# A chunked linear-attention stage: two more key blocks transposed by TensorE, and the order of the stage planned anew

## The chip, the cores and the metric

The kernel runs on one core of a Trainium2 chip. The metric is the device time of one execution in microseconds; lower is better. Three executions of the kernel before took 582.23, 582.09 and 578.52 us, with a median of 582.09 us.

## What is computed

Three stages follow each other. The change lies in the first, a delta-rule linear attention over 2 batches, 8 heads, 768 steps and a head dimension of 48:

```python
k_n = k / (np.linalg.norm(k, axis=-1, keepdims=True) + 1e-06)
for t in range(S):
    y[:, :, t] = np.einsum('bhd,bhde->bhe', q[:, :, t], state)
    v_old = np.einsum('bhde,bhd->bhe', state, kt)
    state = state + bt * np.einsum('bhd,bhe->bhde', kt, vt - v_old)
```

Its output goes through a mixture of experts (8 experts; the gate and a local gate choose one expert for each token, `relu(x @ w1[e]) @ w2[e]`) and then through a mixer (the real part of two Fourier transforms, a normalization, and a two-layer network with a residual sum).

## The kernel before

**Blocks.** The 768 steps are cut into 24 chunks of 32 steps. Four chunks make a block (`hf` = 0 to 5 in the code), and two blocks make a group (`g` = 0 to 2). Every block holds all 16 batch-and-head pairs. Values are kept as two float16 tiles, a high part and a low part (`KBh`, `KBl`), so a product takes three matmuls (`mm3`, L310).

**What happens to a key block** (`prepK`, L270). The keys are normalized (`norm`, L231; VectorE scales them in L277), split into a high part by ScalarE (L224) and a low part by VectorE (L229) in `parts`, and each part is transposed into a tile `KT` of 128 x 2048 float16. `turn` (L164) does that in one of two ways. Either SyncE's queue issues one DMA transpose (L169), or `turn_pe` (L171) makes 16 TensorE transposes into PSUM (L177) in two halves and evicts each half by ScalarE (L180) or VectorE (L183). The table `TK` (L660) says which blocks go which way. VectorE then copies the transposed keys into a stacked form (`ST`, L308), TensorE forms the Gram matrix (`gram`, L313), and ScalarE evicts it (L323).

**The solve.** When both blocks of a group have their Gram matrices, `solve` (L346) transposes them in 32 x 32 pieces on VectorE (`Gu`, L362) and inverts a triangular system in 31 serial steps of two VectorE instructions each (L371, L373). A last VectorE transpose gives `PT` (L377).

**From the solve to the recurrence.** `prepT` (L381) splits `PT` into a high and a low part and copies these into block-diagonal tiles (`TBh`, `TBl`); a `split` (L325) is one ScalarE conversion (L333), one VectorE subtraction (L335) and eight copies, each by VectorE (L341) or ScalarE (L344). Only one split at a time can hold the buffer `ph`. TensorE multiplies `TB` with the keys into `W`, which ScalarE and VectorE evict (L403, L405). `prepV` (L408) and `prepQ` (L424) prepare values and queries; `prepQ` forms the masked query-key products `M` with the same `split`. Where the table `HOLD` is 1 it uses the `KT` tiles of `prepK`; for blocks 3 and 4 it transposes the keys a second time.

**The recurrence.** `chain` (L488) runs 24 steps for each of the two batches. A step needs `W` and `T` of its block: steps 0 to 7 those of group 0, steps 8 to 15 those of group 1, steps 16 to 23 those of group 2. ScalarE evicts the high part of the update `U` (L513), `low` (L535) makes its low part, either on VectorE (L543) or with one TensorE matmul (L546) and ScalarE (L550), and ScalarE and VectorE evict the state (L530, L556). `out` (L558) makes the outputs and sends them to memory, and `logits` (L602) the gate's scores.

**What sets the order.** The order of instructions on every engine is fixed when the kernel is built, by a planner (`Order`, L47). It simulates the engines with a cost in nanoseconds for every instruction (the number in each `yield`), and whenever a simulated engine is free it takes the waiting instruction of lowest rank. The ranks stand in the table `PR` (L662): `K2` is `prepK` of block 2, `T`, `V`, `Q` likewise, `s0` the solve of group 0, `n0` the normalization. The recurrence has rank 0, outputs rank 1, logits rank `LATE`. With `KEEN` and `SHARE` an engine may be held free: it does not take an instruction if another of a lower rank, at most `KEEN`, is due within `SHARE` times the first one's cost. Where two engines can do the same work, `pick` (L59) takes the one whose queue would let it end first by the planner's costs, to which an entry of `BIAS` is added: `BIAS[0]` for `low` on ScalarE, `BIAS[4]` for a split's copy on VectorE, `BIAS[7]` for an eviction of a transpose on VectorE, `BIAS[5]` and `BIAS[6]` for a load issued by ScalarE or GpSimd. Loads may be issued by ScalarE up to `BOTH` and by GpSimd up to `THREE`. A DMA transpose is planned with 2140 ns of SyncE's queue and with a landing time of 4000 ns behind its issue (L170). `LOADS` (L663) is the order of the loads: `k0`, `k1` are halves of the keys, `v0`, `v1` of the values, `w` the gate weights, `b` beta and `c` the constants. On the chip the engines follow the planned order and wait on semaphores.

Of the kernel before, what the change touches and what calls it, by code (L numbers as in the profile page):

```python
# [46 lines left out]
class Order:  # L47
# [40 lines left out]
    def run(s):  # L88
        while s.heap:
            t,_,x=heapq.heappop(s.heap)  # L90
            s.now=t
            if isinstance(x,str): s.grant(x); continue
            g,pr,y=x; s.pr=pr
            while True:
                if y is None: y=next(g,None)
                if y is None: break
                if isinstance(y,str):
                    if y not in s.flags:
                        s.wait.setdefault(y,[]).append((g,pr,None)); break
                elif y[0]=="+":  # L100
                    if not s.res[y[1]]:
                        w=s.wait.setdefault(y,[]); w.append((g,pr,None)); break
                    s.res[y[1]]-=1
                elif y[0]=="-":
                    w=s.wait.get(("+",y[1]))
                    if w:
                        z=min(w,key=lambda z: z[1]); w.remove(z); s.push(t,z)
                    else: s.res[y[1]]+=1
                elif y[0]=="!": s.set(y[1])
                elif y[0]=="":  # L110
                    if y[1]: s.push(t+y[1],(g,pr,None)); break
                else:
                    s.n+=1
                    heapq.heappush(s.q.setdefault(y[0],[]),(pr,s.n,g,y))
                    s.grant(y[0]); break
                y=None
        left={k:len(v) for k,v in s.wait.items() if v}
        assert not left,left

class Attn:  # L120
# [35 lines left out]
    def dma(s,out,in_,n=475):  # L156

        e=s.o.pick(("Q",n),*(("A",n+35+s.BIAS[5]),)*(s.o.now<s.BOTH),*(("P",1081+s.BIAS[6]),)*(s.o.now<s.THREE))
        yield {"Q":("Q",n,"H"),"A":("A",n+35,"H"),"P":("P",1081)}[e]
# [4 lines left out]
    def turn(s,out,in_,f,pe):  # L164

        if pe: s.o.add(s.turn_pe(out,in_,f),s.o.pr)
        else:
            yield ("Q",2140,0)
            s.nc.sync.dma_start_transpose(out=out,in_=in_.rearrange("p u d -> p (u d)"))  # L169
            s.o.add(s.arrive(f,4000))  # L170
    def turn_pe(s,out,in_,f):  # L171
        for i in range(2):
            r=slice(8*i,8*i+8)
            yield ("+","y")
            p=s.psC.tile([128,8,128],F16,tag="y",name="tp",bufs=2)
            yield ("T",440)
            for u in range(8): s.nc.tensor.transpose(p[:,u],in_[:,8*i+u],s.K["identh"])  # L177
            if s.o.pick(("A",1000),("V",1150+s.BIAS[7]))=="A":
                yield ("A",1000)
                s.nc.scalar.activation(out=out[:,r],in_=p,func=AF.Copy)  # L180
            else:
                yield ("V",1150)
                s.nc.vector.tensor_copy(out=out[:,r],in_=p)  # L183
            yield ("-","y")
        yield ("!",f)
# [84 lines left out]
    def prepK(s,hf,first):  # L270
# [11 lines left out]
        f=f"kT{hf}"  # L282
        yield from s.parts(KT,k,s.KBh[i],s.KBl[i],f,f"K{i}",s.TK[hf],"kT0" if hf==1 else None)
        yield ("!",f)
# [40 lines left out]
    def split(s,src,Bh,Bl,z):  # L325
# [10 lines left out]
        for q in range(4):  # L336
            r=slice(32*q,32*q+32)
            for t,B in ((hi,Bh),(lo,Bl)):
                if s.o.pick(("V",245+s.BIAS[4]),("A",640))=="V":
                    yield ("V",245)  # L340
# [83 lines left out]
    def prepQ(s,hf,first):  # L424
# [28 lines left out]
        else:  # L453
            yield ("+","KT")
            KT=[s.pk.tile([128,16,128],F16,tag=f"KT{j}",name=f"KT{j}",bufs=2) for j in range(2)]
            for X,B,x in zip(KT,(s.KBh,s.KBl),"hl"): yield from s.turn(X,B[hf%s.NB],f"kA{hf}{x}",s.TK[hf])
            for x in "hl": yield f"kA{hf}{x}"
# [77 lines left out]
    def low(s,b,c,x,uh,ul):  # L535

        nc=s.nc
        yield ("",600)
        if s.o.pick(("V",524),("A",480+400+s.BIAS[0]))=="V":
            yield ("V",524)  # L540
# [17 lines left out]
    def out(s,b,c,uh,ul):  # L558
# [34 lines left out]
        if hf==5: s.o.add(s.logits_end(b,c,yb),1)  # L593
        elif c8==3: s.o.add(s.logits(b,hf,yb),s.LATE)
        if c8==3:
# [55 lines left out]
    def rest(s):  # L651

        for f in ("ku3","G5","PT2","W43","W53","V4","V5","M4","M5"): yield f
        yield from s.after(s.o)
    BOTH=20000
    KEEN,SHARE=0,0.2
    LATE=20
    THREE=30000
    HOLD=(1, 1, 1, 0, 0, 1)
    TK=(1, 0, 0, 0, 0, 0)  # L660
    BIAS=(-355, -160, 902, 0, 281, 507, 387, 0)
    PR={'K0': 0, 'T0': 11.02, 'V0': 22.82, 'Q0': 10.02, 'K1': 4.12, 'T1': 15.34, 'V1': 12.1, 'Q1': 9.56, 'K2': 13.7, 'T2': 0, 'V2': 12.77, 'Q2': 26.59, 'K3': 7.84, 'T3': 35.68, 'V3': 7.09, 'Q3': 18.76, 'K4': 17.47, 'T4': 0, 'V4': 0, 'Q4': 4.01, 'K5': 55.99, 'T5': 17.02, 'V5': 23.22, 'Q5': 7.29, 's0': 9.74, 's1': 4.18, 's2': 11.55, 'n0': 0, 'n1': 8.98, 'n2': 14.57, 'lq': 5.83, 'lv': 3.01}  # L662
    LOADS="k0 w v0 b c k1 v1"  # L663
    def run(s):
        o=s.o
        s.clear()
        P=lambda n,d: s.PR.get(n,d)
        def loads():
            for n in s.LOADS.split():
                if n=="c": yield from s.load_consts()  # L670
                elif n=="w": yield from s.load_gates()
                elif n=="b": yield from s.load_beta()
                else: yield from s.load(n[0]+"p",int(n[1]))
# [59 lines left out]
class Rest:  # L733
# [687 lines left out]
    KEEN,SHARE=3,0.7  # L1421
# [22 lines left out]
IN=("q","k","v","beta","moe_w_gate","moe_w_local","moe_w1","moe_w2","moe2_w_ch1","moe2_w_ch2")  # L1444
LATE=("rc","upper","mirror")

def program(tc,I,y):
# [4 lines left out]
    def right(n): return pools(name=n,bufs=1,side="right",reuse_waits="tile")  # L1452
    with ExitStack() as st:
# [11 lines left out]
        with tc.manual_schedule():  # L1465
# [7 lines left out]
            def after(o):  # L1473
                eR.close()
                e,lp=right("late"); st.push(e)
                for n in LATE:
                    K[n]=lp.tile(list(I[n].shape),I[n].dtype,name=n)
# [54 lines left out]
```

## Time and profile before

| | |
|---|---|
| median of three runs | 582.09 us |
| the profiled execution's own time | 581.5 us |
| its span, first to last instruction | 579.7 us |
| VectorE (DVE) busy | 422.4 us (73%) |
| TensorE (PE) busy | 469.6 us (81%) |
| ScalarE (ACT) busy | 322.4 us (56%) |
| mean granted TensorE clock | 0.916 |

One execution is profiled. A span is the time from the first to the last instruction. The stretches are cut in microseconds from the span's start. An engine's idle time is put down to the instruction or transfer that released the instruction behind it. The attention's last instructions run at about 241 us; the experts and the mixer fill the rest.

### The profile page before, as it was taken

How to read it: one execution, taken by the hardware profiler on the slowest of the kernel's cores; microseconds unless marked ns; L12 is line 12 of the kernel's file. 1: busy time of each engine (PE TensorE's matmuls, PEld its weight loads, DVE VectorE, ACT ScalarE, POOL GpSimd, SP SyncE). 2: the span in 40 equal slices, each digit the busy share in tenths (PEclk: the TensorE clock that was granted, in tenths of full speed). 3: DMA queues.
4: the chain of work that ended last, by engine and by line, in shares of the span. 5: the costliest groups of instructions: out<-in, count | busy, mean ns of one | idle time of the engine just before them, and what ended most of it. 6: DMA issues, size and time to landing. Idle time of an engine off the chain costs nothing.

```text
span 579.7 us, 12919 instructions
## 1 busy us (share of the span) xinstructions
PE 469.6 (81%) x5172; PEld 373.2 (64%) x5172; DVE 422.4 (73%) x943; ACT 322.4 (56%) x729; POOL 78.6 (14%) x85
## 2 busy tenths in 40 slices
PE   0632026896599799679999999998899999999997
PEld 0531015885488688568888888887787655555575
DVE  7958989898999987479887979878987643231132
ACT  4654337897789998716766666762554332111111
POOL 6000000000000000040343332224111210000010
PEclk9975556997599999979999999999999999999999
DMA  7264035086105103839999997227100000010010
GB/s 250 57 126 119 5 68 74 9 185 132 36 3 103 29 3 91 308 103 356 387 302 321 352 305 246 104 70 267 58 0 1 28 2 1 0 55 0 1 55 27
DMA packets 66991, 67.23 MB, mean 116 GB/s; under 512 B 40086, under 2 KB 59483, under 8 KB 66928
## 3 DMA queue, kind: packets, MB, share of 16 engines
q1 hardware_dynamic: 63936, 57.59, 33.6%
q0 software_dynamic: 2992, 8.79, 4.7%
q8 instruction: 41, 0.67, 0.5%
q14 instruction: 22, 0.18, 0.1%
HBM read 51.95 MB, written 7.67 MB: 103 GB/s over the span
## 4 chain that ended last, share of the span: by engine, by line
PE 27%; issue 18%; POOL 5%; DVE 3%; DMA 1%; ACT 1%; POOLq 0%; ACTq 0%; SPq 0%
PE mp L1377 12%; PE mop L1403 12%; POOL xg L905 3%; POOL x2d L943 2%; PE fp L1243 1%; PE yp L1212 1%; DMA xa<-x2d 1%; PE up L1324 1%; DVE d L1131 1%; DVE zl L1196 1%; ACT zh L1194 0%; DMA x2d<-ot,sim 0%; DVE e L1131 0%; DVE Y L1269 0%; ACT un L1308 0%
## 5 line engine op out<-in xcount | busy, mean ns | idle before, releaser
L1387 DVE SCALAR_TENSOR_TENSOR ml<-mp,mh 128x256 f16<-128x256 f32 (+1 forms) x48 | 26.8, 557 | 81.0 <-ACT mh L1385 80.9
L1377 PE MATMUL mp<-uT,ws 128*128 128x256 f16 (+1 forms) x432 | 77.8, 326 | 0.0
L1403 PE MATMUL mop<-ws,mh 128*128 128x384 f16 x288 | 77.7, 326 | 0.0
L1385 ACT ACTIVATE mh<-mp 128x256 f16<-128x256 f32 (+1 forms) x48 | 23.5, 489 | 89.8 <-PE mp L1377 89.6
L934 PE MATMUL op<-ws,hh 128*128 128x384 f16 (+1 forms) x256 | 67.5, 326 | 0.0
L922 PE MATMUL hp<-xT,ws 128*128 128x240 f16 x576 | 64.6, 266 | 1.0 <-DVE xT L913 0.5
L312 PEld LDWEIGHTS <-KT 128*128 128x128 f16 x576 | 27.2, 117 | 52.8 <-issue 41.5
L922 PEld LDWEIGHTS <-ws 128*128 128x128 f16 x576 | 56.2, 98 | 6.9 <-issue 1.3
L1377 PEld LDWEIGHTS <-ws 128*128 128x128 f16 x432 | 42.2, 98 | 27.2
L898 DVE SCALAR_TENSOR_TENSOR ws<-raw,ws 128x1536 f16<-128x1536 f32 x32 | 55.9, 1749 | 0.0
L312 PE MATMUL ga<-ST,KT 128*128 128x64 f16 x288 | 16.8, 229 | 45.2 <-DVE ST L308 39.0
L895 ACT ACTIVATE ws<-raw 128x1536 f16<-128x1536 f32 x32 | 47.3, 1485 | 0.0
L1403 PE MATMUL mop<-ws,ml 128*128 128x384 f16 x144 | 46.9, 326 | 0.0
L934 PE MATMUL op<-ws,hl 128*112 128x384 f16 (+1 forms) x128 | 41.7, 326 | 0.0
L1403 PEld LDWEIGHTS <-mh 128*128 128x128 f16 x288 | 28.2, 98 | 17.8
L905 POOL DMA_INDIRECT xg<-xd,gm x16 | 22.0, 1377 | 114.7 <-DVE fl L1067 107.7
L934 PEld LDWEIGHTS <-hh 128*128 128x128 f16 (+1 forms) x256 | 29.1, 114 | 11.6
L373 DVE TENSOR_TENSOR P<-P,tmp 128x31 f32<-128x31 f32 (+15 forms) x93 | 31.5, 339 | 1.7
L371 DVE TENSOR_TENSOR tmp<-Gu,P 128x31 f32<-128x31 f32 (+15 forms) x93 | 31.2, 336 | 1.6
L925 DVE SCALAR_TENSOR_TENSOR hl<-hp,hh 128x480 f16<-128x480 f32 x32 | 21.0, 655 | 14.5 <-ACT hh L924 12.9
L943 POOL DMA_INDIRECT x2d<-ot,sim x16 | 19.6, 1228 | 87.5 <-ACT ot L939 85.0
L924 ACT ACTIVATE hh<-hp 128x480 f16<-128x480 f32 x32 | 18.1, 566 | 20.7 <-PE hp L922 18.4
(276 smaller groups left out, 1170.5 us busy)
## 6 DMA issues: line engine op xcount, KB each, us to landing
raw<-moe_w SPq DMA_DIRECT2D x64, 384.0 KB
x<-moe_w_ch SPq DMA_DIRECT2D x24, 384.0 KB
qp<-q SPq DMA_DIRECT2D x5, 512.0 KB
kp<-k SPq DMA_DIRECT2D x6, 384.0 KB
vp<-v SPq DMA_DIRECT2D x6, 384.0 KB
xd<-yb SPq DMA_DIRECT2D x48, 48.0 KB
xa<-x2d SPq DMA_DIRECT2D x6, 384.0 KB
ur<-x2d SPq DMA_DIRECT2D x2, 768.0 KB
```

The source lines that it names most:

```text
L312: s.nc.tensor.matmul(out=out,lhsT=st[l],rhs=mv[m],start=(first and i==0),stop=True,skip_group_check=True)
L371: nc.vector.tensor_tensor(out=x,in0=Gu[:,k,k+1:32].unsqueeze(2).to_broadcast([128,m,n]),in1=P[:,k,0:n].unsqueeze(1).to_broadcast([128,m,n] ...
L373: nc.vector.tensor_tensor(out=P[:,k+1:32,0:n],in0=P[:,k+1:32,0:n],in1=x,op=ALU.subtract)
L895: s.nc.scalar.activation(out=s.W[q][:,0].rearrange("p s c -> p (s c)"),in_=s.raw[q],func=AF.Copy,scale=WS)
L898: s.nc.vector.scalar_tensor_tensor(out=W[1],in0=s.raw[q],scalar=WS,in1=W[0],op0=ALU.mult,op1=ALU.subtract)
L905: nc.gpsimd.indirect_dma_start(out=s.xg[e][t][0:w],out_offset=None,in_=s.xd,in_offset=bass.IndirectOffsetOnAxis(ap=s.gi[0:w,8*t+e:8*t+e+1] ...
L922: nc.tensor.matmul(out=p[:,i],lhsT=s.W[q][:,a,i,128*k:128*k+128],rhs=xT[b][:,k],start=(n==0),stop=(n==8)); n+=1
L934: nc.tensor.matmul(out=s.po[t][0:w],lhsT=hs[a][:,i,128*t:128*t+w],rhs=s.W[q][:,b,i,384:768],start=(g==0 and i==0 and n==0),stop=(g==3 and ...
L943: i=s.nc.gpsimd.indirect_dma_start(out=s.x2d,out_offset=bass.IndirectOffsetOnAxis(ap=s.si[0:w,c:c+1],axis=0),in_=ot,in_offset=None,bounds_ ...
L1377: for k in range(3): nc.tensor.matmul(out=p,lhsT=s.w_ch1(a,k,f),rhs=s.uT[g][b][:,k,0:N],start=(n==0),stop=(n==8)); n+=1
L1387: nc.vector.scalar_tensor_tensor(out=hl,in0=p,scalar=0.0,in1=hh,op0=ALU.max,op1=ALU.subtract)
L1403: nc.tensor.matmul(out=pm[t],lhsT=hs[a][:,128*t:128*t+128],rhs=s.w_ch2(b,f),start=(f==0 and n==0),stop=(f==11 and n==2))
```

## The change

Blocks 1 and 2 are transposed by TensorE instead of by DMA (`TK`). The planned landing time of a DMA transpose becomes 7600 ns for block 0, 7000 ns for block 1 and 5000 ns for the others and for the second transposes in `prepQ`. The ranks, the biases, `KEEN`, `SHARE`, `LATE`, `BOTH` and the order of the loads get new values, so the planner writes another order for the attention. No instruction's form is new.

```diff
-            s.o.add(s.arrive(f,4000))
+            s.o.add(s.arrive(f,(7600,7000,5000)[min(int(f[2]),2)] if f[1]=="T" else 5000))
...
-    BOTH=20000
-    KEEN,SHARE=0,0.2
-    LATE=20
+    BOTH=10000
+    KEEN,SHARE=3,0.17
+    LATE=2
...
-    TK=(1, 0, 0, 0, 0, 0)
-    BIAS=(-355, -160, 902, 0, 281, 507, 387, 0)
-    PR={'K0': 0, 'T0': 11.02, 'V0': 22.82, 'Q0': 10.02, 'K1': 4.12, 'T1': 15.34, 'V1': 12.1, 'Q1': 9.56, 'K2': 13.7, 'T2': 0, 'V2': 12.77, 'Q2': 26.59, 'K3': 7.84, 'T3': 35.68, 'V3': 7.09, 'Q3': 18.76, 'K4': 17.47, 'T4': 0, 'V4': 0, 'Q4': 4.01, 'K5': 55.99, 'T5': 17.02, 'V5': 23.22, 'Q5': 7.29, 's0': 9.74, 's1': 4.18, 's2': 11.55, 'n0': 0, 'n1': 8.98, 'n2': 14.57, 'lq': 5.83, 'lv': 3.01}
-    LOADS="k0 w v0 b c k1 v1"
+    TK=(1, 1, 1, 0, 0, 0)
+    BIAS=(-968, -265, 917, 1203, 0, 646, 0, -72)
+    PR={'K0': 0, 'T0': 23.64, 'V0': 25.4, 'Q0': 5.26, 'K1': 3.26, 'T1': 3.87, 'V1': 23.15, 'Q1': 5.13, 'K2': 11.08, 'T2': 0, 'V2': 25.77, 'Q2': 20.56, 'K3': 17.27, 'T3': 42.07, 'V3': 20.29, 'Q3': 11.99, 'K4': 36.81, 'T4': 11.59, 'V4': 22.21, 'Q4': 3.06, 'K5': 9.48, 'T5': 7.31, 'V5': 24.68, 'Q5': 37.18, 's0': 27.62, 's1': 13.09, 's2': 20.94, 'n0': 2.59, 'n1': 22.39, 'n2': 14.57, 'lq': 0.11, 'lv': 4.13}
+    LOADS="k0 c b v0 w k1 v1"
```

## Rows read from the trace of the kernel before

**Rows 1.** Busy time by stretch: us, its length, then busy us (instructions) of each engine.

```profile
core 0: us, PE busy (x) PEld busy (x) DVE busy (x) ACT busy (x) POOL busy (x), PEclk, DMA share, GB/s
28.70:53.70 25.00, 5.72 (x100) 4.97 (x101) 17.23 (x38) 12.40 (x24) 0.00 (x0) 0.64 0.62 144
53.70:84.70 31.00, 5.63 (x94) 5.10 (x93) 28.61 (x77) 10.89 (x22) 0.95 (x1) 0.50 0.15 34
84.70:141.60 56.90, 42.43 (x812) 38.99 (x813) 51.69 (x133) 47.52 (x146) 0.00 (x0) 0.86 0.48 85
141.60:192.20 50.60, 39.93 (x746) 36.87 (x744) 47.09 (x125) 42.84 (x133) 1.23 (x1) 0.80 0.27 59
...
209.00:237.00 28.00, 26.88 (x571) 24.87 (x569) 19.62 (x62) 23.46 (x87) 0.00 (x0) 1.00 0.39 116
```

**Rows 2.** Timeline of VectorE: start, us, line, out<-in, count, idle before and releaser.

```profile
40.52 1.93 DVE L362 STREAM_TRANSPOSE Gu<-G 128x1024 f32<-128x1024 f32 x1 [0.79 <-ACT G L323]
...
81.01 1.25 DVE L377 STREAM_TRANSPOSE PT<-P 128x1024 f32<-128x1024 f32 x1
...
140.29 1.23 DVE L377 STREAM_TRANSPOSE PT<-P 128x1024 f32<-128x1024 f32 x1
...
190.93 1.25 DVE L377 STREAM_TRANSPOSE PT<-P 128x1024 f32<-128x1024 f32 x1
```

**Rows 3.** Timeline of ScalarE, first update with group 1 (step 8, both batches).

```profile
159.82 1.01 ACT L513 ACTIVATE U<-ups 64x96 f16<-64x96 f32 x4
```

**Rows 4.** Timeline of VectorE from 28.7 to 53.7 us, instructions with idle time before.

```profile
32.76 0.86 DVE L308 COPY ST<-KT 64x1024 f16<-64x1024 f16 x2 [4.06 <-DMA KT<-KBh]
34.33 0.86 DVE L308 COPY ST<-KT 64x1024 f16<-64x1024 f16 x2 [0.71 <-DMA KT<-KBl]
...
37.54 0.69 DVE L335 TENSOR_TENSOR pl<-am,ph 128x512 f16<-128x512 f32 x1 [0.49 <-ACT ph L333]
...
51.62 0.42 DVE L308 COPY ST<-KT 64x1024 f16<-64x1024 f16 x1 [1.22 <-DMA KT<-KBl]
```

**Rows 5.** Timeline of SyncE's queue: block 1's two DMA transposes.

```profile
24.37 1.73 SPq L169 DMA_TRANSPOSE KT<-KBh  x1
26.75 5.51 SPq L169 DMA_TRANSPOSE KT<-KBl  x1
```

**Rows 6.** Timeline: block 0's transposes on TensorE, their evictions by ScalarE and VectorE.

```profile
15.13 1.89 PE L177 MATMUL tp<-ca,KBha 128*128 128x128 f16 x16 [15.13 <-ACT KBha L224]
...
16.20 1.94 ACT L180 ACTIVATE KT<-tp 128x1024 f16<-128x1024 f16 x2 [0.40 <-PE tp L177]
...
21.02 0.63 DVE L183 COPY KT<-tp 128x1024 f16<-128x1024 f16 x1
```

**Rows 7.** Waits of VectorE from 84.7 to 141.6 us: us, times, longest.

```profile
DVE ST L308 <- DMA KT<-KBla: 1.2, 1, 1.2
```

**Rows 8.** Low parts on VectorE and split copies, up to 192.2 us: count, ns min/median/max.

```profile
L543 DVE SCALAR_TENSOR_TENSOR U<-ups,U x18: 243/256/261, 96.2 to 178.6; 64x96 f16<-64x96 f32 x18
...
L341 DVE COPY TBl<-pl x10: 274/284/290, 84.5 to 159.4; 32x512 f16<-32x512 f16 x10
...
L344 ACT ACTIVATE TBh<-ph x12: 612/627/629, 83.7 to 157.1; 32x512 f16<-32x512 f16 x12
L344 ACT ACTIVATE MBl<-pl x9: 608/612/628, 41.0 to 170.8; 32x512 f16<-32x512 f16 x9
L344 ACT ACTIVATE MBh<-ph x8: 625/626/629, 40.5 to 169.3; 32x512 f16<-32x512 f16 x8
L344 ACT ACTIVATE TBl<-pl x6: 608/626/630, 86.5 to 150.0; 32x512 f16<-32x512 f16 x6
```

**Rows 9.** Low parts on VectorE from 209 to 237 us; ScalarE's conversion for block 5.

```profile
L543 DVE SCALAR_TENSOR_TENSOR U<-ups,U x26: 239/256/261, 211.0 to 236.6; 64x96 f16<-64x96 f32 x26
...
206.11 1.08 ACT L333 ACTIVATE ph<-PT 128x512 f16<-128x512 f32 x1
```

## The prediction

> **What bounds the kernel now.** Read first the busy time by stretch. The attention ends at about 241 us, and everything behind it (routing, experts, mixer) keeps its code, so the question is when the attention ends. VectorE is busy 28.61 of 31.00 us, 51.69 of 56.90 and 47.09 of 50.60 in the three stretches from 53.7 to 192.2 us, but only 17.23 of 25.00 us from 28.7 to 53.7; behind 192.2 TensorE takes over (26.88 of 28.00 us from 209 to 237) [rows 1].
>
> Read next the landmarks on VectorE: the loop of 31 steps that solves a group of key blocks is one serial chain. Its first input is ready at 40.52 us, and the solved groups come at 81.01, 140.29 and 190.93 us, with the transposes of 1.23 to 1.25 us that end them [rows 2]. The state recurrence on the other engines waits for those: the first update that uses group 1 runs at 159.82 us, 18.3 us behind the end of its solve (140.29 + 1.23) [rows 2, 3]. So VectorE's own queue, up to the third landmark, sets the end: what it idles ahead of 192 us is lost, and what is taken off it is gained.
>
> Read last who made VectorE idle in the thin stretch. Block 1's DMA transposes: 4.06 us for the high half, 0.71 for the low half; block 2's low half: 1.22 us; behind block 1 come 0.49 us (ScalarE) and 0.79 us (the Gram matrix, on the first landmark's row) [rows 2, 4]. That is 7.27 of the 7.77 us that the stretch lacks (25.00 - 17.23). The high transpose of block 1 was issued at 24.37 us and its first reader started at 32.76, 8.4 us later [rows 4, 5]; the planner allowed 4.0.
>
> **The change part by part.**
>
> *Blocks 1 and 2 are turned by TensorE.* Four DMA transposes go. With them go the waits of block 1 (4.06 + 0.71) and block 2 (1.22): 6.0 us. Of the 1.28 us behind block 1 I take half, since the Gram matrix still has to be formed behind the last copy: together -6.6 us, between 0 (the wait returns in another form) and -7.3. SP's queue loses its part as well: the transpose at 26.75 us held it for 5.51 us [rows 5], and the second key load and the query loads behind it start sooner; nothing waits for these at that place, so I count nothing.
>
> What is added: four tiles, each 16 transposes. Block 0 shows the price: a tile took TensorE 1.89 us, ScalarE 0.97 us for one of the two evictions (1.94 for two), VectorE 0.63 us where it took one [rows 6]. TensorE's 4 x 1.89 = 7.6 us and ScalarE's part lie where these engines have room: 5.72 and 12.40 us busy of 25.00 [rows 1]. If that cover is gone the whole of a tile is on the path, 1.89 + 0.97 us. VectorE's part is on the path: one of block 0's four evictions was its own, so two of the eight: +1.3 us, between 0 and 8 x 0.63 = +5.0.
>
> For one 128x128 block the row gives 1.89/16 = 0.118 us. [...]
>
> *The planner's landing times* (4.0 us become 7.0 for block 1, 5.0 for the other blocks and the late key transposes). Only blocks 3 to 5 still use them for their first turn. Block 5's low half made VectorE wait 1.2 us [rows 7]; a plan that allows 5.0 instead of 4.0 puts other work there: -0.6 us, half of it, between 0 and -1.2.
>
> *The choice of engine.* The bias for the low part of U falls from -355 to -968: before, the planner saw 524 for VectorE and 525 for TensorE with ScalarE; now it sees 524 and -88. The bias for the copies of the splits falls from 281 to 0: VectorE's way looks 281 cheaper. The two pull VectorE in opposite directions. Ahead of 192.2 us VectorE makes 9 low parts (18 instructions of 0.256 us): at most -4.6 us. ScalarE makes 35 split copies there, which cost VectorE 0.28 us each: at most +9.9 us [rows 8]. The low's threshold moves by 613, more than the 0.51 us of a low, the copies' by 281, one copy's length: if 6 lows leave (-3.1) and 8 copies come (+2.3), the net is -0.8 and smaller than what I know of either; I take 0, and both ends for the range.
>
> *The ranks.* The first solve falls behind nearly everything (9.74 to 27.62). It runs in gaps already: from 40.52 to 81.01 us VectorE is all but full [rows 1, 2], so another order of the same work ends at the same time; 0. Block 4's T goes from first (0) to 11.59 and block 5's stands ahead of it at 7.31. Block 5's split cannot start before block 4's has released the buffer `ph`; what remains is a copy already running when block 4's tiles want the engine, half of a 0.63 us copy [rows 8], +0.3 us; if block 5's conversion goes first, the upper end is its 1.08 us [rows 9]. Logits move from rank 20 to 2. They use TensorE and ScalarE only, and the recurrence waits for a solve twice, so ahead of 192 us they are hidden by that wait; 0, without cover a share of the last stretch, which is the slow case below. The waiting rule (KEEN 3, SHARE 0.17) holds back an engine for a higher-ranked instruction that is due within 0.17 of the next one's length, less than before for rank 0, and new for ranks up to 3: 0. The constants are loaded second instead of last, and the ACT queue is open for loads only until 10 us: the first landmark needs block 1's chain, which the earlier constants don't shorten: 0.
>
> **Sum.** -6.6 + 1.3 - 0.6 + 0.3 = -5.6 us. The profiled execution took 581.5 us, so 575.9; the median of the three runs stands 0.6 above it (582.09), so **576.5 us**.
>
> **The rivals.**
>
> *The wait comes back on TensorE (no change).* Two tiles of block 1 and one eviction take 2 x 1.89 + 0.97 = 4.75 us if TensorE gets to them only when VectorE has run out of work, which is today's 4.06 + 0.71 = 4.77. For it: the low half is made last, so one tile at least is always behind it; and Gram matrices want TensorE at the same time. Against it: the high tile can be turned while VectorE makes the low half. With four evictions on VectorE (2.5): -1.2 - 0.6 + 2.5 - 0.6 + 0.3 = +0.4, 582.5 us.
>
> *VectorE is relieved too (a larger gain).* All 9 early low parts leave VectorE, few copies come, and the whole of the 1.28 us goes: -5.6 - 4.6 - 0.6 = -10.8, 571.3 us. For it: the low's bias moved most. Against it: ScalarE is 47.52 of 56.90 us and 42.84 of 50.60 us busy there [rows 1], so the planner will often find it occupied.
>
> *The new biases load the engine that is already full (slower).* In the last eight steps ScalarE is busy 23.46 of 28.00 us [rows 1], and all 13 low parts there (26 instructions) are VectorE's [rows 9]. Moved to ScalarE they cost 0.51 us each (1.01 us for two in rows 3), 6.6 us, while its idle time is 4.5 us of waits in a serial chain that need not shrink. It decides once more than 9 of the 13 move. With half of the 35 copies on VectorE ahead of that (+5.0): -5.6 + 6.6 + 5.0 = +6.0, 588.1 us. For it: the threshold of 613 is more than a low. Against it: the planner counts ScalarE's queue before it chooses.
>
> That the change doesn't do what it says has little room: blocks 1 and 2 keep their turned tiles for the queries, so no second DMA transpose of them is left.
>
> **How the numbers follow.** Forecast 0.40, no change 0.22, larger gain 0.22, slower 0.16. What this kernel's measurement can tell from no change is about 1%, 5.8 us; the forecast lies on that line, and I count 0.22 of it as faster and 0.18 as the same. Faster 0.22 + 0.22 = 0.44, same 0.18 + 0.22 = 0.40, slower 0.16. The range reaches past the larger gain (571.3) by the rest of its bound and stops inside the slow case: 569 to 587 us. The likeliest case's own range is 574 (no eviction on VectorE, block 5's wait and the waits behind block 1 gone: -1.3 - 0.6 - 0.7) to 580 (all eight evictions on VectorE: +3.7).
>
> **What would show it.** Right: no VectorE wait for a transposed tile between 28 and 52 us, the first landmark at 34 to 36 instead of 40.5 us, the third near 185, and the attention's end earlier by the same 5 to 6 us. Wrong in the first step: VectorE idles 4 us again, now for TensorE or an eviction. Wrong in the biases: VectorE's busy time up to the third landmark moves by more than 2 us. Slow case: ScalarE full and TensorE thinner in the last eight steps. All of it is wrong if the third landmark moves and the end does not, or if the stretch behind the attention changes its length.

## The result and the profile after

The changed kernel takes 585.41 us (median of 13 runs, 583.62 to 586.67) against 582.21 us for the kernel before (13 runs beside it): ratio 1.0057, 95% interval 1.004 to 1.0074. It is 3.2 us slower, where 5.6 us less was forecast. That is 0.6%, less than the 1% that I had named as the least that can be told from no change; but the interval leaves out 1, so the kernel is slower, if by little.

The profiled execution has a span of 584.0 us (before 579.7). Read the two attentions side by side first, cut at the same instructions: start of the first solve, ends of the three solves, first instruction of the routing behind the attention. The columns are those of [rows 1]. First the kernel before:

```profile
0.00:40.52 40.52, 13.74 (x200) 12.46 (x201) 30.62 (x63) 21.23 (x34) 10.53 (x27) 0.92 0.53 142
40.52:82.26 41.74, 6.98 (x120) 6.11 (x119) 38.84 (x98) 15.48 (x30) 0.00 (x0) 0.52 0.31 79
82.26:141.52 59.26, 42.35 (x810) 38.91 (x811) 52.95 (x135) 49.80 (x150) 0.95 (x1) 0.85 0.46 82
141.52:192.18 50.66, 39.99 (x747) 36.94 (x745) 47.12 (x125) 42.91 (x133) 1.23 (x1) 0.80 0.27 60
192.18:241.13 48.95, 43.32 (x893) 38.92 (x890) 35.63 (x105) 42.43 (x133) 0.00 (x0) 1.00 0.35 108
```

Then the kernel after, the same view:

```profile
0.00:43.56 43.56, 17.31 (x228) 15.63 (x229) 34.34 (x68) 27.90 (x43) 9.19 (x23) 0.93 0.32 108
43.56:82.86 39.30, 8.77 (x159) 8.03 (x157) 37.54 (x99) 13.64 (x25) 0.00 (x0) 0.59 0.21 58
82.86:140.36 57.50, 41.87 (x762) 38.34 (x762) 50.60 (x127) 48.97 (x149) 0.95 (x1) 0.83 0.35 77
140.36:195.70 55.34, 42.89 (x807) 39.74 (x808) 50.55 (x134) 41.13 (x138) 0.95 (x1) 0.81 0.36 62
195.70:245.84 50.14, 45.70 (x896) 41.70 (x893) 30.99 (x89) 40.83 (x146) 0.00 (x0) 0.93 0.35 111
```

Add the first four rows. VectorE was busy 169.5 us up to the end of the third solve and idle 22.7 of 192.2; now it is busy 173.0 us and idle 22.7 of 195.7. So it has 3.5 us more work and no less idle time. (Another profile of before's order, below, idles 19.8 us up to there, so of the idle time this says only that it did not shrink.) The last row adds 1.2 us at a lower granted clock (0.93 for 1.00), and behind the routing's first instruction the two are alike (584.0 - 245.84 = 338.2 us, before 338.6). VectorE's landmarks, which answer to [rows 2], come 3.0 us later, 0.6 later, 1.2 earlier and 3.5 later. Two stretches grew, the first by 3.0 us and the third solve's by 4.7 (55.3 for 50.7), with VectorE busy 3.7 and 3.4 us more in them; the two between them shrank.

```profile
43.56 1.94 DVE L362 STREAM_TRANSPOSE Gu<-G 128x1024 f32<-128x1024 f32 x1 [0.44 <-ACT G L323]
...
81.61 1.25 DVE L377 STREAM_TRANSPOSE PT<-P 128x1024 f32<-128x1024 f32 x1
...
139.12 1.24 DVE L377 STREAM_TRANSPOSE PT<-P 128x1024 f32<-128x1024 f32 x1
...
194.45 1.25 DVE L377 STREAM_TRANSPOSE PT<-P 128x1024 f32<-128x1024 f32 x1
```

What VectorE waited for from 28.7 to 53.7 us, beside the last wait above, is the answer to [rows 4] (timeline of VectorE, after):

```profile
33.10 0.69 DVE L183 COPY KT<-tp 128x1024 f16<-128x1024 f16 x1 [3.26 <-PE tp L177]
...
35.00 0.42 DVE L308 COPY ST<-KT 64x1024 f16<-64x1024 f16 x1 [0.25 <-ACT KT L180]
```

No DMA is named any more, but 3.26 us stand where 4.06 stood: VectorE now waits for TensorE. The timeline of TensorE after shows why; it answers to the first row of [rows 6]:

```profile
27.18 1.03 PE L177 MATMUL tp<-ca,KBh 128*128 128x128 f16 x8 [1.73 <-ACT KBh L224]
29.90 1.03 PE L177 MATMUL tp<-ca,KBl 128*128 128x128 f16 x8 [1.68 <-DVE KBl L229]
30.72 1.48 PE L312 MATMUL ga<-SQ,KT 128*128 128x64 f16 x24
32.02 1.04 PE L177 MATMUL tp<-ca,KBh 128*128 128x128 f16 x8
32.86 1.05 PE L177 MATMUL tp<-ca,KBl 128*128 128x128 f16 x8
```

A tile of block 1 isn't turned in 1.89 us as block 0's was in before. Its second eight transposes wait behind the first eight of the other tile and behind query products of block 0, so the high tile takes from 27.18 to past 33 us. And both parts of block 1 come later than before. VectorE makes the low part, here in after and in before's order (the best version below, where L240 is L229):

```profile
28.82 1.02 DVE L229 SCALAR_TENSOR_TENSOR KBl<-kp,ca,KBh 128x768 f16<-128x768 f32 x1
```

```profile
25.90 0.99 DVE L240 SCALAR_TENSOR_TENSOR KBl<-kp,ca,KBh 128x768 f16<-128x768 f32 x1
```

The low part is done at 29.84 us in after. In before the DMA transpose that reads it was issued at 26.75 [rows 5], 3.1 us sooner. That is as much as the first solve is late (3.0 us).

VectorE's extra work is read from the groups by line and shape, up to the end of the third solve (busy us, mean ns). Before, then after:

```profile
L543 DVE SCALAR_TENSOR_TENSOR U<-ups,U 64x96 f16<-64x96 f32 x18 | 4.6, 253 | 0.2
L341 DVE COPY TBl<-pl 32x512 f16<-32x512 f16 x10 | 2.8, 283 | 0.2
L341 DVE COPY MBl<-pl 32x512 f16<-32x512 f16 x7 | 2.7, 390 | 0.1
L341 DVE COPY MBh<-ph 32x512 f16<-32x512 f16 x8 | 2.3, 282 | 0.2
L341 DVE COPY TBh<-ph 32x512 f16<-32x512 f16 x4 | 1.1, 285 | 0.1
```

```profile
L420 DVE SCALAR_TENSOR_TENSOR V<-vp,V 128x768 f16<-128x768 f32 x6 | 5.7, 944 | 0.0
L341 DVE COPY TBl<-pl 32x512 f16<-32x512 f16 x13 | 3.7, 283 | 0.3
L341 DVE COPY MBl<-pl 32x512 f16<-32x512 f16 x12 | 3.4, 284 | 0.3
L341 DVE COPY MBh<-ph 32x512 f16<-32x512 f16 x11 | 3.1, 282 | 0.2
L341 DVE COPY TBh<-ph 32x512 f16<-32x512 f16 x9 | 2.6, 286 | 0.3
...
L543 DVE SCALAR_TENSOR_TENSOR U<-ups,U 64x96 f16<-64x96 f32 x4 | 1.0, 255 | 0.3 <-ACT U L513 0.3
```

Seven low parts left (14 instructions, -3.6 us) and sixteen split copies came (29 to 45, +3.9). So the two choices of engine nearly cancel, +0.3 us. One more `V` (five before) adds 0.9 and one more eviction of a turned tile 0.8; these four make 2.0 of the 3.5 us. Three more memsets (L210) add 0.4, and one instruction of the normalization (L266) took 0.89 us for 0.24. All durations of VectorE up to there add up to 190.0 us, before 187.3; the rest of the 3.5 us is that consecutive instructions overlap less (17.0 us, before 17.8).

### The profile page after: what moved, and what is told of

The parts are those of the page before. It is cut to its first block, busy times and chain, and to the rows that moved or that the text cites. A ratio compares the mean times of both kernels' runs of the same rounds, so it can differ in the third digit from the quotient of the medians.

```text
span 584.0 us, 13058 instructions
## 1 busy us (share of the span) xinstructions
PE 479.5 (82%) x5255; PEld 383.2 (66%) x5255; DVE 420.6 (72%) x933; ACT 323.8 (55%) x750; POOL 77.5 (13%) x81
## 4 chain that ended last, share of the span: by engine, by line
PE 30%; issue 15%; POOL 5%; DVE 4%; ACT 1%; POOLq 0%; ACTq 0%
PE mp L1377 12%; PE mop L1403 12%; POOL xg L905 3%; POOL x2d L943 2%; PE fp L1243 2%; PE hp L922 1%; DVE ws L898 1%; PE yp L1212 1%; PE op L934 1%; PE up L1324 1%; DVE zl L1196 1%; DVE e L1131 0%; ACT zh L1194 0%; DVE d L1131 0%; ACT un L1308 0%
## 5 line engine op out<-in xcount | busy, mean ns | idle before, releaser
L312 PE MATMUL ga<-ST,KT 128*128 128x64 f16 x288 | 14.7, 217 | 36.5 <-DVE ST L308 33.2
L1403 PEld LDWEIGHTS <-mh 128*128 128x128 f16 x288 | 28.2, 98 | 17.8
```

What stands on the lines that cost most here:

```text
L312: s.nc.tensor.matmul(out=out,lhsT=st[l],rhs=mv[m],start=(first and i==0),stop=True,skip_group_check=True)
L1403: nc.tensor.matmul(out=pm[t],lhsT=hs[a][:,128*t:128*t+128],rhs=s.w_ch2(b,f),start=(f==0 and n==0),stop=(f==11 and n==2))
```

## The experiments

In the experiments marked *in place* the planner writes the same order as for its parent, and only the named instructions are changed when they are emitted. The other three are planned anew. A profile is one execution: before's order reaches the end of the third solve at 192.18 us in one profile and at 189.09 in another (the padded kernel below), while VectorE's busy time there differs by 0.2 us only. So I lean on busy times and on medians. Landmarks and idle times of single profiles differed by 3 us here with VectorE's work the same.

**The turn alone, in before's order** (in place).

```diff
+            s.o.add(s.turn_in_place(out,in_))        # f is kT1 or kT2: no dma_start_transpose
+    def turn_in_place(s,out,in_):
+        for i in range(2):
+            ...
+            for u in range(8): s.nc.tensor.transpose(p[:,u],in_[:,8*i+u],s.K["identh"])
+            yield ("",1000)
+            s.nc.scalar.activation(out=out[:,r],in_=p,func=AF.Copy)
```

> The kernel before with its order on every engine unchanged; only the four DMA transposes of blocks 1 and 2 are replaced, at the same place in the order, by 16 TensorE transposes and two ScalarE evictions each. Theory (turning on TensorE is worth it, the new order of the changed kernel loses it): block 1's tiles are there at about 27.5 and 30.5 us instead of 32.8 and 34.3, VectorE's waits of 4.06 + 0.71 + 1.22 us shrink to 2 us or less, the first solve starts near 37 us instead of 40.5, and the execution is 3 to 5 us shorter than the kernel before (577 to 579 us). Rival (turning on TensorE takes as long as the DMA transposes): the first solve starts within 0.7 us of 40.5 and the time stays within 1 us of the kernel before. Third reading (the 64 transposes and 8 evictions delay ScalarE or TensorE elsewhere): slower than the kernel before.

Measured: 580.6 us, ratio 0.9996 (0.9967 to 1.0026). The first solve starts at 38.16 us (before 40.52), the third ends at 188.05 (192.18), and the attention ends 3.5 us earlier. But the part behind it is 2.7 us longer (341.3 for 338.6): TensorE's conditional branch behind the routing, which skips the code for overflowing experts, took 3.69 us instead of 0.36.

> e1 (the order of before, blocks 1 and 2 turned by TensorE in place) with 24 instead of 20 filler products on TensorE ahead of the overflow branch, which also moves all later code of TensorE. In e1 the attention ended 3.5 us earlier but TensorE's branch took 3.69 us where the kernel before has 0.36, and the clock fell behind it. Theory (the branch's length is an accident of where TensorE's code stands or of the moment): the branch takes about 0.4 us again and the execution is 3 to 4 us shorter than the kernel before (578 to 579 us). Rival (an earlier end of the attention makes the branch wait for something that is not earlier): the branch ends at the same time as in e1, and the total stays within 1 us of e1.

Measured (`WARMR`, the fillers ahead of that branch, 20 to 24): 580.05 us, 0.9966 (0.9948 to 0.9985); the branch again 3.74 us. Moving it by eight matmuls changed nothing, so the theory as put there fell. I then counted TensorE's records up to the branch in every trace, which gave the next three.

```diff
-    WARMR=20
+    WARMR=16
```

> The order of before with blocks 1 and 2 turned in place, as in the earlier run, but with 16 instead of 20 fillers ahead of TensorE's branch behind the routing (8 matmuls less). Position theory: what the branch costs goes by how many instructions TensorE has had in front of it (its records up to the branch, weight loads included): 5,783 gave 0.35 us twice, 5,790 and 5,806 gave 3.7 us, 5,825 to 5,865 gave 0.46 us; in the two long ones the transfer of TensorE's next 16 KB of instructions starts 1.0 to 1.3 us behind the start of the branch, in the short ones it had been there, or the jump stayed in front of it. With 5,774 the branch takes 0.35 us and the kernel 3 us less than with 20 fillers: 577.3 us, 5 us below before. Rival (the branch is long because TensorE reaches it early, or because of the order): 3.7 us again and 580 to 581 us.

Measured: **576.83 us**, ratio 0.9923 (0.9898 to 0.9948), 4.5 us faster than before, and the best version of this study. The branch takes 0.35 us. The routing begins 4.6 us earlier (236.56 for 241.13 us) and the part behind its first instruction is as long as before's (338.2 for 338.6), so the gain lies in the attention and not in the four fillers fewer.

```diff
+            if hf==3 and c==3:
+                for _ in range(10): nc.tensor.matmul(out=s.SB[0][:,256:512],lhsT=s.K["identh"],rhs=s.K["idents"],...)
```

> The same kernel with 20 fillers, and 20 more matmuls in the last stretch of the attention (ahead of the waiting gate transposes of block 3), as in the run on the order of after: 5,830 instructions ahead of the branch. Position theory: the branch takes 0.46 us, 577 to 578 us, if the added matmuls (2.5 us of TensorE) lie in waits; up to 1 us more if they don't. Rival (not position): 3.7 us and 580.5 us or more.

Measured: 580.54 us, 0.998 (0.996 to 1.0). The branch takes 0.46 us as expected, the time is 2.5 us above the 578 that I gave, and 1.5 above the 579 for matmuls that don't lie in waits: from the end of the third solve to the routing's first instruction it takes 51.3 us instead of 49.6 without the added matmuls, so in this order they did not lie in waits.

```diff
+            if f=="kT0h" and i==0:
+                pad=s.psC.tile([128,64],F32,tag="u",name="pad",bufs=2)
+                for _ in range(67): s.nc.tensor.matmul(out=pad,lhsT=s.K["identh"],rhs=s.K["identh"][:,0:64],...)
```

> The kernel before, with 67 narrow matmuls more ahead of the first transposes, where TensorE has had nothing to do, so that 5,794 instructions lie ahead of the branch; nothing else changed, the tile they write is not used. Position theory: the branch takes 3.7 us instead of 0.36, and the kernel 582.2 + 3.3 = 585.5 us with the attention's end unmoved. Rival (not position): 0.36 us and 582 us.

Measured: 582.87 us, 1.002 (1.0002 to 1.0037): slower, but by 1.2 us and not 3.3. The branch takes 4.13 us, and behind the routing's first instruction the kernel is 2.7 us longer (341.2 for 338.6); the attention ended 1.6 us earlier in the profiled execution, which I can't tell from the spread. These are the branches of before, of the turn in place with 20, 16 and 20 + 20 matmuls, and of the padded kernel (view of the line of the `If`: ns, start; the lines shift with the edits):

```profile
L994 PEldq COMPARE_BRANCH  x1: 358/358/358, 255.0 to 255.0; - x1
```

```profile
L1005 PEldq COMPARE_BRANCH  x1: 3687/3687/3687, 251.5 to 251.5; - x1
```

```profile
L1005 PEldq COMPARE_BRANCH  x1: 352/352/352, 249.2 to 249.2; - x1
```

```profile
L1008 PEldq COMPARE_BRANCH  x1: 460/460/460, 255.6 to 255.6; - x1
```

```profile
L997 PEldq COMPARE_BRANCH  x1: 4127/4127/4127, 254.0 to 254.0; - x1
```

The position theory gave the three durations beforehand: 0.35, 0.46 and 3.7 us were expected, 0.35, 0.46 and 4.13 measured. The turn on TensorE isn't slow: with the branch at 0.35 us the kernel takes 576.83 us. Its 64 transposes and their weight loads moved the branch from behind 5,660 records of TensorE, where it took 0.36 us, to behind 5,790, where it took 3.69. VectorE's account for the best version, cut like the two above, shows the turn's own gain; its busy time is before's, its idle time 18.6 us up to the end of the third solve (before 22.7 in one profile, 19.8 in the other):

```profile
0.00:37.63 37.63, 13.39 (x222) 12.07 (x223) 30.63 (x62) 24.98 (x38) 10.55 (x27) 1.00 0.37 124
37.63:78.80 41.17, 10.65 (x166) 9.87 (x163) 38.83 (x98) 19.70 (x34) 0.00 (x0) 0.50 0.20 56
78.80:137.66 58.86, 42.34 (x849) 39.06 (x850) 52.84 (x135) 50.71 (x152) 0.95 (x1) 0.86 0.38 81
137.66:187.91 50.25, 37.86 (x713) 34.92 (x708) 47.02 (x125) 42.20 (x131) 1.23 (x1) 0.83 0.35 62
187.91:236.56 48.65, 43.33 (x893) 38.92 (x890) 35.64 (x106) 42.15 (x133) 0.00 (x0) 1.00 0.36 113
```

**The new order alone** (in place, on the order of after): blocks 1 and 2 turned by DMA again.

```diff
+        if f[:3] in ("kT1","kT2"):
+            ...
+            if not i: s.nc.sync.dma_start_transpose(out=out,in_=in_.rearrange("p u d -> p (u d)"))
```

> The order of after, with blocks 1 and 2 turned by DMA again, in place: each of the four tiles by one transpose on SyncE's queue where its first eight TensorE transposes stood; the 64 TensorE transposes and 8 evictions go. This is the fourth cell: old order with DMA 582, old order turned by TensorE 577 (with the branch short), new order turned by TensorE 585, new order with DMA is this one. TensorE has 5,697 instructions ahead of its branch, so 0.36 us. If turning gives in the new order what it gave in the old (4 to 5 us), 589 to 590 us, and the new order by itself costs 7 to 8 us. Rival: in the new order the turn on TensorE gained next to nothing, since it came late and piecewise (VectorE still waited 3.3 us for it): 584 to 587 us, and the loss of after is the order's 3.5 us of VectorE work with no gain to set against it.

Measured: 585.2 us, 1.0049 (1.0027 to 1.007). The rival holds: in the new order the turn on TensorE is worth nothing (585.2 against 585.4). VectorE's waits for block 1 (timeline of VectorE, then of SyncE's queue):

```profile
31.53 0.86 DVE L318 COPY ST<-KT 64x1024 f16<-64x1024 f16 x2 [1.36 <-DMA KT<-KBh]
34.32 0.42 DVE L318 COPY ST<-KT 64x1024 f16<-64x1024 f16 x1 [1.94 <-DMA KT<-KBl]
```

```profile
27.52 1.99 SPq L176 DMA_TRANSPOSE KT<-KBh  x1
30.20 1.56 SPq L176 DMA_TRANSPOSE KT<-KBl  x1
```

1.36 + 1.94 = 3.3 us, about what the piecewise turn on TensorE made VectorE wait. The DMA transposes were read 4.0 and 4.1 us behind their issue (27.52 to 31.53, 30.20 to 34.32), against 8.4 and 7.6 us in before [rows 4, 5]. They were issued 3.2 and 3.5 us later than in before (24.37, 26.75), so the first solve, at 42.35 us, still starts later than before's: the order itself brings block 1 late. With DMA VectorE is busy 171.6 us up to the end of the third solve, 2.1 more than before; the other 1.4 us of after are its two evictions of turned tiles.

**Parts of the new order** (in place, on the order of after).

```diff
-                    nc.vector.tensor_copy(out=B[r,:,r],in_=t[r])
+                    if give: give-=1; nc.scalar.activation(out=B[r,:,r],in_=t[r],func=AF.Copy)   # give: 3 per T, 2 per M, blocks 2 and 3
+                    else: nc.vector.tensor_copy(out=B[r,:,r],in_=t[r])
```

> The changed kernel with its order unchanged; 10 of the 24 split copies that its plan gives to VectorE during the third solve (blocks 2 and 3) are made by ScalarE at the same place in the order. Theory (VectorE is the bound up to the end of the third solve, so the copies' bias costs 10 x 0.28 us there): the third solve ends 2.5 to 3 us earlier than at 195.7 us and the execution is 2 to 3 us shorter than the changed kernel. Rival (the stretch is long for another reason, the recurrence or ScalarE): the third solve ends within 1 us of 195.7 and the time stays within 1 us of the changed kernel, or rises, since ScalarE gets 6.3 us more.

Measured: 584.37 us, 1.0046 (1.0016 to 1.0076). VectorE's busy time up to the third solve's end falls by 2.2 us (to 170.8), the landmark by 1.4, the median by 1.0. By VectorE's account the copies are a part of the loss, at the landmark of about half the size expected. A median 1.0 us lower, of six runs, is not clear of the spread (583.0 to 586.0 us), so no run shows what they cost in time.

The edit with 20 matmuls ahead of the gate's transposes, shown above, on the order of after:

> The changed kernel with its order unchanged; 20 matmuls that only keep TensorE busy (they add a block of zeros into unused columns as the kernel's own ten do) are put in front of the two gate transposes of block 3 that wait for ScalarE at 198 to 200.5 us. Theory (TensorE stands idle there, its granted clock falls from 1.00 to 0.50 and the W tiles of block 4 run at the lower level): the clock stays 1.00 from 198 to 210 us, the first state update of block 4 comes about 12.5 us behind the third solve instead of 14.4, and the execution is 1.5 to 2.5 us shorter than the changed kernel. Rival (the W tiles wait for the copies of the split anyway): the update comes at the same place within 0.5 us, and the time stays within 1 us.

Measured: 583.95 us, 1.0034 (1.0019 to 1.005). From the third solve's transpose to the routing it takes 49.7 us instead of 51.4. Read TensorE in the last stretch of after (timeline of TensorE and ScalarE, then busy time by stretch):

```profile
199.61 0.31 PE L609 MATMUL lps<-ca,yb 128*96 128x128 f32 x1 [1.50 <-ACT yb L590]
200.54 0.67 PE L609 MATMUL lps<-ca,yb 128*96 128x128 f32 x4 [0.62 <-ACT am L323]
...
202.41 2.31 PE L480 MATMUL S<-ca 128*128 128x256 f16 x10
...
207.00 0.60 ACT L403 ACTIVATE WT<-wps 128x512 f16<-128x512 f32 x1 [3.32 <-PE wps L312]
```

```profile
198.00:201.00 3.00, 0.88 (x7) 0.51 (x5) 2.93 (x9) 2.89 (x10) 0.00 (x0) 1.00 0.15 35
201.00:207.00 6.00, 6.00 (x70) 5.00 (x69) 3.85 (x9) 2.68 (x7) 0.00 (x0) 0.50 0.22 51
```

TensorE is busy 0.88 of 3.00 us, waiting for the inputs of gate scores, which now rank ahead, and then its granted clock is 0.50 just where block 4's `W` is made. With the fillers the same views read:

```profile
203.68 1.26 PE L480 MATMUL S<-ca 128*128 128x256 f16 x10
...
206.16 0.60 ACT L403 ACTIVATE WT<-wps 128x512 f16<-128x512 f32 x1 [1.21 <-PE wps L312]
```

```profile
198.00:201.00 3.00, 1.56 (x19) 1.28 (x16) 2.63 (x8) 2.86 (x10) 0.00 (x0) 1.00 0.07 18
201.00:207.00 6.00, 5.93 (x116) 5.35 (x115) 4.54 (x11) 3.85 (x8) 0.00 (x0) 1.00 0.25 59
```

The next edit puts the second eight transposes of a tile right behind the first eight:

```diff
+            if i==0:
+                ps=[s.psC.tile([128,8,128],F16,tag=g,name="tp",bufs=2) for g in "yu"]
+                for u in range(16): s.nc.tensor.transpose(ps[u//8][:,u%8],in_[:,u],s.K["identh"])
+            p=ps[i]
```

> The changed kernel with its order unchanged except on TensorE: the second 8 transposes of each tile of blocks 0, 1 and 2 follow the first 8 at once, into a second PSUM buffer, and not at the place that the plan gives them behind the first half's eviction. Theory (the changed plan's first solve is late because halves stand in TensorE's queue behind others that wait: block 0's second high half behind the low half, block 1's behind a Gram product): block 0's and block 1's turned tiles are complete 1 to 3 us earlier, the first solve starts 1.5 to 3 us earlier than at 43.6 us and the execution is 1 to 3 us shorter than the changed kernel. Rival (the start is late because VectorE's and ScalarE's other work, query products and block 2, is ranked in front): the first solve starts within 0.7 us of 43.6.

Measured: 583.73 us, 1.0037 (1.0016 to 1.0059); a tile takes 1.89 us again, and the first solve starts at 43.29 us (43.56). So it isn't the split of the tile that holds that solve back: VectorE now waits 4.0 us (0.48 + 3.55) for ScalarE's evictions of the tiles, whose parts come as late as in after. The three edits together:

> The order of after with the three edits tried singly put together: ten split copies back on ScalarE (-1.0 us in the median), 20 matmuls ahead of the waiting gate transposes (-1.5), the second eight transposes of a turned tile right behind the first eight (-1.7). If the three places of loss are separate: 585.4 - 4.2 = 581.2 us, at or just below before. If they overlap (the two that act before the end of the third solve share its chain): 582 to 583.5 us.

Measured: 584.18 us, 1.0043 (1.0026 to 1.0061). That misses both ranges that I gave, 1.2 us below after. The sum of the single medians (4.2 us) was too much for edits of 1 to 1.7 us: VectorE's busy time is down to 171.0 us, its idle time up to 23.6.

**Planned anew with one parameter back or alone.** On after, eight transposes planned with 950 ns, then before's `BIAS`; on before, only the new `TK`:

```diff
-            yield ("T",440)
+            yield ("T",950)
```

> The changed kernel planned anew with one number changed: a group of 8 TensorE transposes is planned with 950 ns instead of 440 (the trace has 1.01 to 1.06 us). Theory (the plan is late in the first 45 us because it takes the turning for half as long as it is and queues Gram matrices and further transposes behind it): the first solve starts 1.5 to 3 us earlier than at 43.6 us, and the execution is 1 to 3 us shorter than the changed kernel. Rival (the price is not the cause; the ranks are): the first solve starts within 0.7 us of 43.6. As the whole order is written anew from that point, the end can move by some us either way without telling the two apart; the first solve's start is what counts.

```diff
-    BIAS=(-968, -265, 917, 1203, 0, 646, 0, -72)
+    BIAS=(-355, -160, 902, 0, 281, 507, 387, 0)
```

> The changed kernel with the old BIAS, planned anew. Theory (the new biases put 10 more split copies on VectorE during the third solve and cost 2 to 3 us there): the third solve lasts 46 to 48 us instead of 49.7, and the execution is 1.5 to 3 us shorter than the changed kernel (582.5 to 584). Rival (the length of the third solve comes from the ranks): it lasts 49 us or more, and the time stays at 585 or above.

```diff
-    TK=(1, 0, 0, 0, 0, 0)
+    TK=(1, 1, 1, 0, 0, 0)
```

> The kernel before with the table TK alone changed (blocks 1 and 2 by TensorE), planned anew with the old ranks, biases and landing times. Theory (the turning is a gain when the ranks are the old ones): the first solve starts at 39 us or earlier, the third ends at 188 us or earlier, 577 to 580 us. Rival (turning as the planner writes it, in serial halves, is late whatever the ranks): first solve at 41 us or later and a time at or above the kernel before.

Measured: 590.87 us (1.0167, 1.0133 to 1.0201), 599.61 us (1.0308, 1.0273 to 1.0342) and 597.08 us (1.0271, 1.0235 to 1.0307). One parameter changed by itself costs 5 to 15 us. None did what I hoped. With 950 ns, close to the 1.03 us measured, the first solve still starts at 43.22 us (43.56) and the kernel is slower, which speaks against the planned price as the cause. With before's biases the third solve takes 52 us, not 46 to 48, so the biases alone are not what made it long. With the new `TK` alone the first solve starts at 40.2 us and the third ends at 209.2, 21 us behind what I expected; the order was written anew there too, so this says nothing of the turn by itself. VectorE's account (busy time up to the end of the third solve's transpose, the rest of that stretch, device time):

| kernel | VectorE busy | idle | us |
|---|---|---|---|
| turn in place, 16 fillers | 169.3 | 18.6 | 576.8 |
| before | 169.5 | 22.7 | 582.2 |
| new order, DMA | 171.6 | 23.1 | 585.2 |
| after | 173.0 | 22.7 | 585.4 |
| after, 950 ns | 175.8 | 21.2 | 590.9 |
| after, before's biases | 178.5 | 24.2 | 599.6 |
| before, new `TK` | 181.4 | 27.8 | 597.1 |

## Why the prediction was wrong

**What bounds the kernel: right for these orders.** In the first four rows of the table the device time follows VectorE's busy and idle time added, to 1.6 us, and the part behind the attention kept its length in after. In the last three rows it doesn't: there the stretch from the third solve to the routing changed too (54, 54 and 46 us, in before 49).

**The turn, -6.6 us: right in mechanism in the order it was read from, worth nothing in the other.** In before's order it gave 4.5 us (3.0 to 5.9), once the branch was off its bad place, at 576.8 us: about two thirds of the term, with all evictions on ScalarE. That 576.8 is near the forecast of 576.5 is a coincidence; it is another kernel. The turn's price on VectorE, +1.3 us, was +0.8 in after. The first solve, which I had put at 34 to 36 us, starts at 37.3 to 39.5 in place (before 40.5) and at 43.56 in after. The waits were removed on paper from a trace whose order the change also rewrote. In the new order the DMA transposes were read 4.0 and 4.1 us behind their issue, and the turn came piecewise and as late, so taking the DMA out gained nothing. What I called the rival "the wait comes back on TensorE" is what happened, with 3.26 + 0.25 us.

**The ranks, put at 0: the step that failed.** The reason given was that "another order of the same work ends at the same time". The new order without the turn takes 585.2 us, 0.5% (1.6 to 4.1 us) more than before, and has no gain for the turn in it: 585.4 us with it. It ends later because the work is neither the same nor at the same place. VectorE has 2.1 us more of it up to the third solve's end, and block 1's low part comes 3.1 us later, so that the turn starts behind what it was to gain. What the turn lost by it, 4.5 us, and what the order costs, 3.0 us, are most of the 8.8 us between forecast and result.

**The choice of engine, put at 0: right in the net, wrong in both counts.** I guessed 6 low parts gone and 8 copies come. It was 7 and 16, -3.6 and +3.9 us, which nearly cancel. My test for the biases, VectorE's busy time moving by more than 2 us, came out at 3.5, but other work makes most of that; a single total can't tell biases from ranks. The slow rival had the copies right, ahead of 192 us. In the last eight steps 9 of the 13 low parts left VectorE as well (26 to 8 instructions in the 28 us from 213.7), but TensorE was no thinner there (27.22 for 26.88 us), and the whole last stretch grew by 1.2 us, so this half of the rival cost little. That the range of 569 to 587 us holds 585.4 is owed to this rival, which had another cause in mind: luck.

**Logits at rank 2, taken as hidden: 1.2 us.** They opened a gap on TensorE ahead of block 4's `W`, and the granted clock was 0.50 behind it; the fillers, with the clock at 1.00, gave 1.5 us back in the median.

**Block 5's wait (-0.6) and block 4's `T` (+0.3)** were not separable from this in any run, and are too small to be told from the spread. What stays open is which of the ranks and loads make block 1's parts late and give VectorE the extra work: no run changes one of them in place. The three edits to the new order brought 1.2 us of 3.2 together, and the first solve's start, 3 us later than before's, hardly moved with any of them; none of them touches the parts.

## What to carry to other kernels

When a change lets a planner write the order again, a sum over the old trace prices only the mechanism, not the kernel: apply the mechanism to the old order first and measure that, then the new order without it. Of a new order, count the work that it gives the bounding engine up to the landmark that ends last; here it was 3.5 us more, and the waits that went came back elsewhere. Look also at when the inputs of the faster step are ready: here the step started 3 us later and gained nothing (585.4 us against 585.2). And before a conditional branch is passed by, look at what it costs in both traces: here it took 0.35 to 4.13 us, by how many records of TensorE lay ahead of it.

## What the runs showed of the hardware

**A branch of TensorE that took 0.35 to 4.13 us, by how much code lay ahead of it.** With 5,660 to 5,783 records of TensorE up to it (weight loads and its sequencer's records counted) it took 0.35 to 0.36 us, with 5,789 to 5,806 it took 3.7 to 4.1, with 5,824 and more 0.46; the fifteen traces fall into these three groups. In the turn in place with 20 fillers the queue q8, which the DMA view names `instruction`, has no transfer from 240 us to the branch at 251.5, and one while the branch lasts (DMA view of 251.5 to 255.2 us):

```profile
q8 instruction: 1, 0.02, 1.9%
```

In the padded kernel it is the same. In after, at 0.46 us, q8 has a transfer ahead of the branch and none during it. In before, at 0.36 us, it has none from 250 us to the branch's end at 255.4 and one by 258, so there the branch ended without it. That q8 is TensorE's and that the long branch waited for the transfer is read from the order of events, not measured by itself. In before q8 moved 0.67 MB in 41 transfers, 16 KB each. The shortest of the fifteen branches took 352 ns.

**DMA transposes of one size were read 8.4 and 4.0 us behind their issue.** The same 128 x 2048 tile took 8.4 us from issue to reader in before [rows 4, 5] and 4.0 us in the new order with DMA, so the 4.0 us that before's planner had for it fit the one order and not the other. In before 0.52 MB on queue q0, a load of queries issued by GpSimd, moved between 24.4 and 34.3 us beside block 1's two transposes; in after, whose order the run with DMA keeps, q0 moved nothing between 24.4 and 34.3 us. That this load is what made them late is likely and not shown: no run moves it alone.
